# One VectorE operation per item of the side queue, and constants moved by 64 bytes: a transformer block on one core

## The chip, the cores and the metric

The kernel runs on one core of one Trainium2 chip. The time is the device time of one execution in microseconds (us). The kernel before took 1429.42 us, the median of 3 runs (1429.18 to 1429.70).

## The reference

One pre-norm transformer block in fp32 over 2048 tokens of width 512: attention with 32 query heads of width 16 that share one key and one value head, then a GEGLU feed-forward of width 1792.

```python
h  = x + A(layernorm(x))    # S = 2048, D = 512
h2 = h + B(layernorm(h))    # F = 1792
# A: q = x@wq (32 heads of 16), k = x@wk, v = x@wv (one head),
#    softmax(q k^T / 4) v, then @ wo
# B: (gelu(x @ w_gate) * (x @ w_up)) @ w_down
```

## The kernel before, in words

**Products.** Dense products and scores run in fp32r, each factor split into a high part and a rest, with three products (high x high, high x rest, rest x high) summed in PSUM. For the scores the three parts lie on top of one another in 50 rows (`kaug` holds the keys, `qg` the queries, with two more rows for a bound on the score), so one matmul does all.

**Attention.** The tokens are four blocks `b` of 512 queries, each with 8 groups `g` of 4 heads and 16 key chunks `kc` of 128: 512 units, each two scores (`u` = 0, 1). `scores` (line 345) issues two matmuls for one `u`, on rows 0 to 49 and 64 to 113, which run side by side (L352), and ScalarE takes the exponential into `p` (L356). `weigh` (line 358) multiplies `p` by the values `v_sb`, four heads in four column groups (L360; the profile counts each matmul twice). After 16 chunks `evacuate` copies the sum out (`oT`, L373) and it is turned around through DRAM and divided (L389, L398 to L409).

**Dense work of the block before, woven in.** From the middle of the second block on, the loop at lines 1069 to 1093 walks 47 lists of three cycles (`CYCLES`, line 45), 141 cycles in all. In a cycle the letter s issues a score, d one step of dense work, and v (or the count at the cycle's start) products with `v_sb`. Where too little dense work is ready, the cycle is idle: it takes its `plain` letters, without d, and `before(idle)` empties the side list.

`queue_products` lists the dense products of a block: `project` (with `wo`, tiles pp), then for each of 14 chunks `f` of 128 columns `up` for gate and up (pg, pu), with `down` (pd) of chunks 0 to 3 and 4 to 7 woven in two chunks after the last of them, and the rest at the block's end. `rows(a)` (line 732) runs the list twice: `rows(0)` on partitions 0 to 63 of both factors, `rows(1)` on 64 to 127, six steps later (`LAG`). The matmuls of the two streams run side by side. A product is 12 steps (fewer for some `down`), L751. Each takes a PSUM bank from `spare`, which holds three. At its last step `done` evacuates it on VectorE: L621 copies the first half out of PSUM, L625 adds the second, L681 adds to `h` for `down`, L574 and L577 for `project`.

**The side queue.** Other VectorE work of the dense part stands in the list `later`. `side(n)` (line 540) takes up to `n` items off its front and issues them. It is called with 2 after each `done` (line 758) and once a cycle in `before` (line 1059). Its items for one `f`: `cube` (L612, L613), a marker that lets ScalarE take the tanh (L637) at the next cycle's start, `weigh_up` (L643, L644), `part` (L125, L126, which make `gh` and `gl`). `norm` and its `scale` stand in the same list. `need(b, f)` issues from the list until `f` is done, where a `down` would read it too early. The order of VectorE and SyncE instructions is that in which the program issues them (`manual_schedule`).

**The tail.** The last block's dense part (`last_dense`, line 797) runs after the attention, on all 128 rows (L781, L836), with no side queue. Its first two `w2` tiles, for chunks 0 to 3, lie in buffers of `p` (line 506), the others in the dense pool (line 508).

**Where tiles lie in SBUF.** A pool's tiles lie one after another in the order of their allocation, each partition's row rounded up to 32 bytes. The pool `const` starts at byte 16512 of a partition: `ident` (512 bytes), `power` (8), `kaug`, `v_sb`, `wo_hi`, `wo_lo`, `q2` (20), `flag` (4), `b1`, `b2`. It ends at 43904, where the pools `early` (first half) and later `dense` begin. The pool of the attention (`p`, `qg`, `oc`, `o_hi`, `o_lo`) lies at the other end, from 153568 on.

Of the kernel before, what the change touches and what calls it, by code (L numbers as in the profile page):

```python
# [9 lines left out]
F32 = mybir.dt.float32  # L10
F32R = mybir.dt.float32r
BF16 = mybir.dt.bfloat16
I32 = mybir.dt.int32
AF = mybir.ActivationFunctionType
ALU = mybir.AluOpType
# [4 lines left out]
P = 128  # L20
# [37 lines left out]
def kernel(  # L58
# [12 lines left out]
    nc = tc.nc  # L71
# [3 lines left out]
    DH = wk.shape[1]  # L75
    H = wq.shape[1] // DH
    F = w_gate.shape[1]
    T = 512
    NT = S // P
    NB = S // T  # L80
# [18 lines left out]
    const = ctx.enter_context(tc.tile_pool(name="const", bufs=1))  # L99
# [5 lines left out]
    nc.vector.memset(power[:, 0:1], -0.5)  # L105
    nc.vector.memset(power[:, 1:2], 0.5)

    kaug = const.tile([P, S], F32R, name="kaug")
    v_sb = const.tile([P, KC, 2 * DH], F32, name="v_sb")
    wo_hi = const.tile([P, DC, D], F32R, name="wo_hi")  # L110
    wo_lo = const.tile([P, DC, D], F32R, name="wo_lo")
    q2 = const.tile([H, NB + 1], F32, name="q2")


    q_d = dram.tile([H, KR, S], F32R, name="q_d")
    acc_d = dram.tile([P, 4, T], F32, name="acc_d")
# [4 lines left out]
    def split(eng_hi, hi, lo, src, eng_lo=None):  # L121
        if eng_hi is nc.scalar:
            nc.scalar.activation(hi, src, AF.Copy)
        else:
            eng_hi.tensor_copy(hi, src)  # L125
        (eng_lo or nc.vector).tensor_tensor(lo, src, hi.bitcast(F32), op=ALU.subtract)  # L126
# [21 lines left out]
    def attend(first):  # L148
        with ExitStack() as outer:
            with tc.manual_schedule(  # L150
                engines={mybir.EngineType.PE, mybir.EngineType.Pool, mybir.EngineType.Activation}
            ):
                run(outer, first)


    def run(outer, first):
# [24 lines left out]
        eb = None  # L181
        if first:
            eb = early.enter_context(tc.tile_pool(name="early", bufs=1))

            xT = {
                b: [eb.tile([P, DC, T], F32R, name=f"xT_{w}_{b}") for w in ("hi", "lo")]
                for b in range(1, NB)
            }
            wq_hi = eb.tile([P, DC, D], F32R, name="wq_hi")
            wq_lo = eb.tile([P, DC, D], F32R, name="wq_lo")  # L190
            sel = eb.tile([P, DC, H], BF16, name="sel")
            k2m = eb.tile([H, 1], F32, name="k2m")


        def project_q(b, cs, eng, col):
# [126 lines left out]
        if first:  # L322
            set_banks("ps_pro")
            width = 8
            order = tc.manual_schedule(engines={mybir.EngineType.DVE})
            with order:
                qg_first = prologue(
                    psum1, xT, wq_hi, wq_lo, sel, k2m, q_first, q_rest, advance,
                    first_q, first_bound, eb
                )  # L330
        sb = outer.enter_context(tc.tile_pool(name="attn", bufs=1, side="right"))
# [163 lines left out]
        def load_w1(i):  # L495
            b, m = divmod(i, 2 * FC)
            if b == NB:
                return
            f, k = divmod(m, 2)
            w = db.tile([P, 2, DC, P], F32R, tag="w1", bufs=3, name=f"w1_{b}_{f}_{k}")  # L500
            nc.sync.dma_start(w.bitcast(F32), w1_d[f, k].bitcast(F32))
            w1s[b, f, k] = w
# [19 lines left out]
        scaled_at, halves, gs, gated = {}, {}, {}, set()  # L522
        tanhs, later = [], []
# [21 lines left out]
        def product_terms(parts):  # L545
            return [
                (l, r, f)
                for f, (lh, ll), (rh, rl) in parts
                for l, r in ((lh, rh), (lh, rl), (ll, rh))
            ]  # L550
# [49 lines left out]
        def up(b, f, k):  # L600
            def terms():
                w = w1s.pop((b, f, k))
                hi, lo = xTs[b]
                return product_terms([
                    (None, (w[:, 0, c, :], w[:, 1, c, :]), (hi[:, c, :], lo[:, c, :]))
                    for c in range(DC)
                ])

            def cube():
                g, a = halves[b, f, 0], db.tile([P, T], F32, tag="ga", bufs=2, name=f"ga_{b}_{f}")  # L610
                halves[b, f, 2] = a
                nc.vector.tensor_tensor(a, g, g, op=ALU.mult)  # L612
                nc.vector.scalar_tensor_tensor(  # L613
                    a, a, 1.0 / GELU_A, g, op0=ALU.add, op1=ALU.mult
                )

            def done(a, bank):
                tag = "gu"[k]
                if a == 0:
                    half = db.tile([P, T], F32, tag=tag, bufs=2, name=f"{tag}_{b}_{f}")  # L620
                    nc.vector.tensor_copy(half, bank)  # L621
                    halves[b, f, k] = half
                else:
                    half = halves[b, f, k]
                    nc.vector.tensor_tensor(half, half, bank, op=ALU.add)  # L625
                    load_w1(b * 2 * FC + 2 * f + k + 3)
                    if k == 0:
                        later.append(cube)
                    else:
                        later.append(lambda: tanhs.append((b, f)))  # L630

            ready = (lambda: turned.get(b, 0) == TB) if f == 0 and k == 0 else None
            return f"p{'gu'[k]}_{b}_{f}", 3 * DC, terms, done, ready

        def bend(b, f):
# [3 lines left out]
        def gate(b, f):  # L639
            g, u, a = (halves.pop((b, f, k)) for k in range(3))  # L640

            def weigh_up():
                nc.vector.scalar_tensor_tensor(a, a, 1.0, g, op0=ALU.add, op1=ALU.mult)  # L643
                nc.vector.tensor_tensor(a, a, u, op=ALU.mult)  # L644

            def part():
                key = b, f // 2
                if key not in gs:
                    gs[key] = [
                        db.tile([P, 2, T], F32R, tag=tag, bufs=3, name=f"{tag}_{b}_{f // 2}")  # L650
                        for tag in ("gh", "gl")
                    ]
                gh, gl = gs[key]
                split(nc.vector, gh[:, f % 2, :], gl[:, f % 2, :], a)
                gated.add((b, f))

            return [weigh_up, part]

        def need(b, f):
            while (b, f) not in gated:  # L660
                if later:
                    side(1)
                else:
                    key = tanhs.pop(0)
                    bend(*key)
                    later.extend(gate(*key))
# [402 lines left out]
        for i in range(-((lead - end) // 16)):  # L1069
            if first and i in BOUND_LISTS:  # L1070
                bound_flag(BOUND_LISTS.index(i))
            for count, woven, plain in CYCLES:
                idle = available() < woven.count("d")
                if idle:
                    while available():
                        step()
                    if at == len(queue) or queue[at][0].startswith("pg"):
                        catch_up()
                bent = before(idle)
                if not idle:  # L1080
                    finish(count)
                for key in bent:
                    later.extend(gate(*key))
                for move in plain if idle else woven:
                    if move == "d":
                        step()
                    elif move == "v":
                        finish(1)
                        clock += 4
                    elif n < end:  # L1090
                        score(n)
                        n += 1
                        clock += 1
# [24 lines left out]
    def prologue(psum1, xT, wq_hi, wq_lo, sel, k2m, q_first, q_rest, advance, first_q, first_bound, eb):  # L1118
        with ExitStack() as pro:
            sb = pro.enter_context(tc.tile_pool(name="pro", bufs=1))  # L1120
            xT[0] = [sb.tile([P, DC, T], F32R, name=f"xT_{w}_0") for w in ("hi", "lo")]

            warm = sb.tile([P, 1], F32, name="warm")
            nc.scalar.activation(warm, power[:, 1:2], AF.Copy)

            wkv = sb.tile([P, DC, 2 * DH], F32, name="wkv")
# [196 lines left out]
            b = NB - 1  # L1323
# [18 lines left out]
                advance(q_rest, 3 * DC * (DC - FIRST_Q) - 21)  # L1342
            return qg

    flag = const.tile([1, 1], I32, name="flag")
    b1 = const.tile([1, 1], F32, name="b1")
    b2 = const.tile([1, H], F32, name="b2")
    b_d = dram.tile([1, H], F32, name="b_d")
# [83 lines left out]
```

## Time and profile before

| What | Value |
|---|---|
| median of 3 runs | 1429.42 us |
| the profiled execution's own time | 1433.01 us |
| its span, first to last instruction | 1430.9 us |
| granted TensorE clock, mean | 0.997 |
| VectorE instructions, busy | 1043, 639.4 us |
| POOL busy | 219.4 us |

The profile is of one execution. Its page has the busy time of each engine (PE is TensorE's matmuls, PEld its weight loads, DVE VectorE, ACT ScalarE, POOL GpSimd), the chain of work that ended last, and the costliest groups of instructions: line, engine, operation, `out<-in` by the tiles' names, the count, busy time and mean length, then the idle time just before them and what ended it. Matmuls are pipelined and their ends are modelled, so a busy PE may still lose time; it is seen in the distance from one start to the next. The trace answers further questions: who waited for whom, the instructions in order of time, the chain in order of time, and the groups of a stretch.

### The profile page before, as it was taken

How to read it: one execution, taken by the hardware profiler on the slowest of the kernel's cores; microseconds unless marked ns; L12 is line 12 of the kernel's file. 1: busy time of each engine (PE TensorE's matmuls, PEld its weight loads, DVE VectorE, ACT ScalarE, POOL GpSimd, SP SyncE). 2: the span in 40 equal slices, each digit the busy share in tenths (PEclk: the TensorE clock that was granted, in tenths of full speed). 3: DMA queues.
4: the chain of work that ended last, by engine and by line, in shares of the span. 5: the costliest groups of instructions: out<-in, count | busy, mean ns of one | idle time of the engine just before them, and what ended most of it. 6: DMA issues, size and time to landing. Idle time of an engine off the chain costs nothing.

```text
span 1430.9 us, 25109 instructions
## 1 busy us (share of the span) xinstructions
PE 1396.5 (98%) x10384; PEld 752.4 (53%) x10384; DVE 639.4 (45%) x1043; ACT 1031.6 (72%) x1147; POOL 219.4 (15%) x305
## 2 busy tenths in 40 slices
PE   6999999999999999999999999999999999999998
PEld 5433333335455555545555555545555555556876
DVE  7413131224364444455364444545354453436665
ACT  7699999997877777877777777777777777752000
POOL 5587767710000000000000000000000000001000
PEclk9999999999999999999999999999999999999999
DMA  4467667634222332312422333311332333244352
GB/s 157 140 204 237 222 216 222 226 103 177 71 90 89 111 116 101 108 64 63 168 82 78 131 101 107 108 49 42 147 101 86 115 112 104 89 148 175 126 185 76
DMA packets 66930, 180.57 MB, mean 126 GB/s; under 512 B 9436, under 2 KB 9436, under 8 KB 66776
## 3 DMA queue, kind: packets, MB, share of 16 engines
q1 hardware_dynamic: 56976, 144.79, 30.4%
q0 software_dynamic: 9760, 34.08, 7.1%
q8 instruction: 84, 1.38, 0.4%
q14 instruction: 38, 0.31, 0.1%
q10 hardware_dynamic: 72, 0.00, 0.0%
HBM read 131.13 MB, written 47.71 MB: 125 GB/s over the span
## 4 chain that ended last, share of the span: by engine, by line
PE 89%; DVE 4%; ACT 3%; DMA 1%; issue 1%; SPq 0%; ACTq 0%; DVEq 0%
PE acc L360 31%; PE s L352 19%; PE pg L751 8%; PE pd L751 8%; PE pu L751 7%; PE pq L205 4%; ACT p L356 3%; PE pd L781 3%; PE pp L751 2%; PE pu L781 2%; PE pg L781 2%; DMA w<-w_d 1%; PE pk L1219 1%; PE pd_rest L793 1%; DVE ga L644 0%
## 5 line engine op out<-in xcount | busy, mean ns | idle before, releaser
L356 ACT ACTIVATE p<-s 128x1024 f32<-128x1024 f32 x1024 | 960.8, 1039 | 241.2 <-PE s L352 240.9
L360 PE MATMUL acc<-p,v_sb 128*32 128x512 f32 x4096 | 492.6, 601 | 0.0
L352 PE MATMUL s<-qg,kaug 50*128 50x512 f32 x1984 | 389.8, 427 | 4.1 <-ACT p L356 3.6
L352 PEld LDWEIGHTS s<-qg,kaug 50*128 50x128 f32 x1984 | 171.6, 184 | 286.8 <-issue 133.0
L360 PEld LDWEIGHTS acc<-p,v_sb 128*32 128x32 f32 x4096 | 110.1, 109 | 231.7 <-issue 217.3
L751 PE MATMUL pg<-x2h,w 64*128 64x512 f32 x672 | 177.1, 394 | 4.2 <-DVE g L625 3.1
L751 PE MATMUL pu<-x2h,w 64*128 64x512 f32 x672 | 175.6, 393 | 0.0
L135 POOL TENSOR_SCALAR rstd<-mv 128x1 f32<-128x1 f32 x16 | 3.5, 220 | 977.9 <-DVE mv L133 977.8
L751 PE MATMUL pd<-w,gh 64*128 64x512 f32 x624 | 124.1, 392 | 1.4 <-DVE h L681 1.4
L681 DVE TENSOR_TENSOR h<-h,pd 128x512 f32<-128x512 f32 x80 | 54.4, 686 | 149.4 <-PE pd L751 149.4
L751 PEld LDWEIGHTS pg<-x2h,w 64*128 64x128 f32 x672 | 95.8, 185 | 20.3 <-DVE g L625 6.5
L751 PEld LDWEIGHTS pu<-x2h,w 64*128 64x128 f32 x672 | 94.7, 185 | 11.4
L751 PE MATMUL pg<-x2l,w 64*128 64x512 f32 x336 | 100.3, 391 | 0.0
L751 PE MATMUL pu<-x2l,w 64*128 64x512 f32 x336 | 99.2, 391 | 0.0
L751 PEld LDWEIGHTS pd<-w,gh 64*128 64x128 f32 x624 | 68.4, 185 | 13.1 <-DVE h L681 2.7
L890 ACT ACTIVATE ga<-ga 128x512 f32<-128x512 f32 x14 | 8.8, 632 | 92.0 <-DVE ga L887 92.0
L389 DVE RECIPROCAL oc<-oc 128x128 f32<-128x128 f32 x64 | 56.6, 922 | 34.2 <-DMA oc<-acc_d 33.8
L751 PE MATMUL pd<-w,gl 64*128 64x512 f32 x312 | 71.8, 391 | 0.0
L625 DVE TENSOR_TENSOR g<-g,pg 128x512 f32<-128x512 f32 x42 | 28.7, 684 | 91.0 <-PE pg L751 91.0
L625 DVE TENSOR_TENSOR u<-u,pu 128x512 f32<-128x512 f32 x42 | 28.9, 687 | 78.7 <-PE pu L751 78.5
L621 DVE COPY g<-pg 128x512 f32<-128x512 f32 x42 | 29.0, 691 | 74.7 <-PE pg L751 74.7
L125 DVE CAST qh<-pq 128x512 fp32r<-128x512 f32 x11 | 7.6, 689 | 114.4 <-PE pq L205 114.4
(242 smaller groups left out, 1477.7 us busy)
## 6 DMA issues: line engine op xcount, KB each, us to landing
w<-w_d SPq DMA_DIRECT2D x112, 512.0 KB
w<-w_d SPq DMA_DIRECT2D x28, 1024.0 KB
qg<-q_d SPq DMA_DIRECT2D x62, 200.0 KB
q_d<-qh SPq DMA_DIRECT2D x32, 256.0 KB
acc_d<-oT SPq DMA_DIRECT2D x32, 256.0 KB
oc<-acc_d SPq DMA_DIRECT2D x128, 64.0 KB
w_d<-w_0b POOLq DMA_DIRECT2D x14, 512.0 KB, 3.8
w_d<-w_1b POOLq DMA_DIRECT2D x14, 512.0 KB, 5.6
```

The lines of the kernel that those rows point to most:

```text
L205: nc.tensor.matmul(pq, wt[:, d, c * P : (c + 1) * P], xt[:, d, :], start=(n == 0), stop=(n == 3 * DC - 1),)
L352: nc.tensor.matmul(s[:, a, :], kaug[rows, kc * P : (kc + 1) * P], qg[rows, u, :], start=True, stop=True,)
L356: nc.scalar.activation(p[:, 2 * u : 2 * u + 2, :], s, AF.Exp, scale=SCALE)
L360: nc.tensor.matmul(acc[32 * j : 32 * j + 32, :], v_sb[:, kc, :], p[:, j, :], start=(kc == 0), stop=(kc == KC - 1), skip_group_check=True,)
L389: nc.vector.reciprocal(oc[:, 1, sl], oc[:, 1, sl])
L621: nc.vector.tensor_copy(half, bank)
L625: nc.vector.tensor_tensor(half, half, bank, op=ALU.add)
L681: nc.vector.tensor_tensor(hs[b, t], hs[b, t], bank, op=ALU.add)
L751: nc.tensor.matmul(bank, lhsT[r], rhs[r], start=(k == 0), stop=(k == n - 1), skip_group_check=True,)
L781: nc.tensor.matmul(bank, lhsT, rhs, start=(i == 0), stop=(i == len(ts) - 1))
L793: nc.tensor.matmul(bank, lhsT, rhs, start=(i == 0), stop=(i == len(ts) - 1))
L1219: nc.tensor.matmul(pks[b], wt[:, c, :], xt[:, c, :], start=(c == 0 and n == 0), stop=(c == DC - 1 and n == 2),)
```

## The change

Two things are changed.

First, the side queue. `cube` becomes two items, `square` (the old L612) and `cube` (L613); `weigh_up` becomes `bring` (L643) and `weigh_up` (L644); `part` becomes `high` (L125) and `low` (L126). Each item is one VectorE operation. `side` still takes two items a call.

Second, the order and width of small tiles. `q2` and `flag` are allocated ahead of `kaug`; `k2m` and `warm` are made 64 bytes wider in the pool, with only their first column used, and `warm` is allocated ahead of `xT[0]`. No instruction is added or removed.

```diff
+    q2 = const.tile([H, NB + 1], F32, name="q2")
+    flag = const.tile([1, 1], I32, name="flag")
     kaug = const.tile([P, S], F32R, name="kaug")
     v_sb = const.tile([P, KC, 2 * DH], F32, name="v_sb")
     wo_hi = const.tile([P, DC, D], F32R, name="wo_hi")
     wo_lo = const.tile([P, DC, D], F32R, name="wo_lo")
-    q2 = const.tile([H, NB + 1], F32, name="q2")
...
-            k2m = eb.tile([H, 1], F32, name="k2m")
+            k2m = eb.tile([H, T // 32 + 1], F32, name="k2m")[:, :1]
...
-            def cube():
+            def square():
                 g, a = halves[b, f, 0], db.tile([P, T], F32, tag="ga", bufs=2, name=f"ga_{b}_{f}")
                 halves[b, f, 2] = a
                 nc.vector.tensor_tensor(a, g, g, op=ALU.mult)
+
+            def cube():
+                g, a = halves[b, f, 0], halves[b, f, 2]
                 nc.vector.scalar_tensor_tensor(
                     a, a, 1.0 / GELU_A, g, op0=ALU.add, op1=ALU.mult
                 )
...
-                        later.append(cube)
+                        later.extend((square, cube))
...
+            def bring():
+                nc.vector.scalar_tensor_tensor(a, a, 1.0, g, op0=ALU.add, op1=ALU.mult)
+
             def weigh_up():
-                nc.vector.scalar_tensor_tensor(a, a, 1.0, g, op0=ALU.add, op1=ALU.mult)
                 nc.vector.tensor_tensor(a, a, u, op=ALU.mult)
 
-            def part():
+            def high():
...
-                gh, gl = gs[key]
-                split(nc.vector, gh[:, f % 2, :], gl[:, f % 2, :], a)
+                nc.vector.tensor_copy(gs[key][0][:, f % 2, :], a)
+
+            def low():
+                gh, gl = gs[b, f // 2]
+                nc.vector.tensor_tensor(
+                    gl[:, f % 2, :], a, gh[:, f % 2, :].bitcast(F32), op=ALU.subtract
+                )
                 gated.add((b, f))
 
-            return [weigh_up, part]
+            return [bring, weigh_up, high, low]
...
+            warm = sb.tile([P, DH], F32, name="warm")[:, :1]
             xT[0] = [sb.tile([P, DC, T], F32R, name=f"xT_{w}_0") for w in ("hi", "lo")]
-            warm = sb.tile([P, 1], F32, name="warm")
...
-    flag = const.tile([1, 1], I32, name="flag")
```

## The prediction, made before the changed kernel was timed

> **What bounds the kernel now.** I read the page first: the head, the row of TensorE, and the shares of the chain that ended last.
>
> ```profile
> span 1430.9 us, 25109 instructions
> PE 1396.5 (98%) x10384; PEld 752.4 (53%) x10384; DVE 639.4 (45%) x1043; ACT 1031.6 (72%) x1147; POOL 219.4 (15%) x305
> PE 89%; DVE 4%; ACT 3%; DMA 1%; issue 1%; SPq 0%; ACTq 0%; DVEq 0%
> L356 ACT ACTIVATE p<-s 128x1024 f32<-128x1024 f32 x1024 | 960.8, 1039 | 241.2 <-PE s L352 240.9
> ```
>
> TensorE is busy 98% of the span and is 89% of the chain. ScalarE, the next busiest, spends 240.9 us waiting for TensorE's scores. VectorE has 55% of the span free. So only what delays TensorE counts, and a VectorE edit is worth what TensorE waits for VectorE. The waits of PE over the stretch in which attention and dense products are woven (300 to 1275 us) give that; columns are total us, times, longest.
>
> ```profile
> PE s L352 <- ACT p L356: 3.6, 10, 0.7
> PE pg L751 <- DVE g L625: 3.1, 8, 0.4
> PE pd L751 <- DVE h L681: 1.4, 3, 0.6
> PE pg L751 <- DVE u L621: 1.2, 2, 0.6
> ```
>
> There are thirteen waits for VectorE, eight of one kind. All are waits for a PSUM bank: three banks (`spare`) serve two streams of products, and a product's first matmul needs the bank that the last evacuation but one gave back. No row has a product waiting for `gh` or `gl`, so gated values are never late.
>
> The rows show idle time against modelled matmul ends; what a wait costs is read from the starts. This is the timeline of PE around one of the eight, then that of DVE before it (start, length, idle in brackets).
>
> ```profile
> 709.33 0.40 PE L352 MATMUL s<-qg,kaug 50*128 50x512 f32 x2
> 709.56 0.40 PE L751 MATMUL pu<-x2l,w 64*128 64x512 f32 x2
> 709.79 0.40 PE L751 MATMUL pu<-x2h,w 64*128 64x512 f32 x2
> 710.57 0.50 PE L751 MATMUL pg<-x2h,w 64*128 64x512 f32 x1 [0.37 <-DVE g L625]
> 710.57 0.50 PE L751 MATMUL pu<-x2h,w 64*128 64x512 f32 x1
> 710.91 0.40 PE L352 MATMUL s<-qg,kaug 50*128 50x512 f32 x2
> ```
>
> ```profile
> 706.71 0.69 DVE L621 COPY g<-pg 128x512 f32<-128x512 f32 x1 [0.17 <-PE pg L751]
> 707.32 0.68 DVE L643 SCALAR_TENSOR_TENSOR ga<-ga,g 128x512 f32<-128x512 f32 x1
> 708.04 0.69 DVE L644 TENSOR_TENSOR ga<-ga,u 128x512 f32<-128x512 f32 x1
> 708.76 0.43 DVE L125 CAST gh<-ga 128x512 fp32r<-128x512 f32 x1
> 709.22 0.69 DVE L126 TENSOR_TENSOR gl<-ga,gh 128x512 fp32r<-128x512 f32 x1
> 709.83 0.68 DVE L625 TENSOR_TENSOR g<-g,pg 128x512 f32<-128x512 f32 x1
> 710.55 0.69 DVE L612 TENSOR_TENSOR ga<-g 128x512 f32<-128x512 f32 x1
> ```
>
> TensorE starts a slot every 0.23 us (709.33, 709.56, 709.79). The next starts 0.78 us on, so 0.55 us are lost, and the one after it 0.34 us on, 0.11 us more: 0.65 us a wait, 5.2 us for eight. The cause stands in the second fence. The evacuation at 706.71 was followed by `side(2)`, and its two items were `weigh_up` (L643, L644) and `part` (L125, L126): four operations, 707.32 to 709.83. The evacuation of `g` (L625) stood behind them with no idle time before it, and its bank came late.
>
> **The side queue, step by step.** No operation is added or removed; the same seven an `f` keep their order among themselves and are dealt out two a call instead of up to four. In the case above the call after the copy at 706.71 now emits L643 and L644 only. L625 then starts where L125 did, at 708.76, 1.07 us earlier. The slot that lost 0.55 us lost it to L625's late end, so it is free 0.5 us before TensorE needs it: **the wait goes whole**, 0.65 us. Next in the queue come L125 and L126 (1.1 us), then the evacuation of `u`, then L612 and L613: a call puts two operations (1.4 us) ahead of the next evacuation, where it put up to four (here 2.5 us).
>
> The two waits for `u` are the same with reciprocals between. DVE, then PE, at the first:
>
> ```profile
> 723.03 0.69 DVE L625 TENSOR_TENSOR g<-g,pg 128x512 f32<-128x512 f32 x1 [2.93 <-PE pg L751]
> 723.64 0.68 DVE L643 SCALAR_TENSOR_TENSOR ga<-ga,g 128x512 f32<-128x512 f32 x1
> 724.36 0.69 DVE L644 TENSOR_TENSOR ga<-ga,u 128x512 f32<-128x512 f32 x1
> 725.08 0.43 DVE L125 CAST gh<-ga 128x512 fp32r<-128x512 f32 x1
> 725.54 0.69 DVE L126 TENSOR_TENSOR gl<-ga,gh 128x512 fp32r<-128x512 f32 x1
> 726.15 1.76 DVE L389 RECIPROCAL oc<-oc 128x128 f32<-128x128 f32 x2
> 727.83 0.63 DVE L612 TENSOR_TENSOR ga<-g 128x512 f32<-128x512 f32 x1
> 728.49 0.69 DVE L613 SCALAR_TENSOR_TENSOR ga<-ga,g 128x512 f32<-128x512 f32 x1
> 729.10 0.68 DVE L621 COPY u<-pu 128x512 f32<-128x512 f32 x1
> ```
>
> ```profile
> 728.63 0.63 PE L751 MATMUL pg<-x2h,w 64*128 64x512 f32 x2
> 729.84 0.50 PE L751 MATMUL pg<-x2h,w 64*128 64x512 f32 x1 [0.58 <-DVE u L621]
> 730.18 0.62 PE L751 MATMUL pg<-x2l,w 64*128 64x512 f32 x2
> ```
>
> The last slot before is at 728.63 + 0.23 = 728.86; 0.98 us to the next and 0.34 to the one after lose 0.75 + 0.11 = 0.86 us. Now L612 and L613 come out one call later, behind the copy of `u`, which moves up by their 1.3 us. I count 0.65 us saved and leave 0.2 for what now follows the copy: 1.3 us for two. The three waits of `pd` for `h` (L681) come from products of six terms whose evacuations follow each other with no item between: unchanged.
>
> Sum: 5.2 + 1.3 = **6.5 us**; the ends are 0 (the waits only move) and 6.9 (all ten go).
>
> What could come late instead: an item is now up to one call further back, so the tanh and `gl` come later by a few microseconds. `gl` of an `f` is first read two `f` later, 48 slots of 0.23 us or more, over 11 us; at a block's end, where less work lies between, a cycle without dense work empties the list (`side(100)`). ScalarE's 240.9 us of waiting cover the tanh. Without that cover a late `gl` would stop TensorE by about what one call holds, 1.4 us, once a block: 4 us. DMAs: none is issued by an item; `load_w1` stays in `done`.
>
> **The layout.** Each tile takes its row's bytes rounded up to 32. `q2` and `flag` (32 bytes each) now lie ahead of `kaug`, so `kaug`, `v_sb`, `wo_hi` and `wo_lo` move up by 64 bytes; the same 64 are gone behind them, so the dense pool (`x2h`, `w`, `gh`, `gl`) and the attention pool (`qg`, `p`, `o_hi`) **don't move**. Row starts modulo 256: `kaug` and `wo` go from 160 to 224, which is where `qg`, `p` and `o_hi` lie; the dense pool stays at 128. `v_sb`'s chunks of 128 bytes alternate 160 and 32, now 224 and 96. In the prologue `xT[0]` goes from 0 to 128, like `wq_hi`, and `qg_first` follows `kaug`.
>
> The trace has one clean trial of such a match: in the last block the first two `w2` tiles sit in `p` buffers (224) and the others in the dense pool (128), with `gh` at 128. The chain shows the two runs of 48 matmuls, and PE's groups of each window its means (first pair of rows the mismatched, second the matched).
>
> ```profile
> 1335.26 11.21 PE pd L781 x48
> 1368.27 10.88 PE pd L781 x48
> ```
>
> ```profile
> L781 PE MATMUL pd<-w,gh 128*128 128x512 f32 x32 | 10.0, 394 | 0.0
> L781 PE MATMUL pd<-w,gl 128*128 128x512 f32 x16 | 6.4, 399 | 0.0
> L781 PE MATMUL pd<-w,gh 128*128 128x512 f32 x32 | 9.9, 389 | 0.0
> L781 PE MATMUL pd<-w,gl 128*128 128x512 f32 x16 | 6.2, 389 | 0.0
> ```
>
> The mismatch costs (11.21 - 10.88)/48 = **6.9 ns a matmul**. In the woven part, where two row groups run side by side, the mismatched `pp` and the matched `pd` take the same; these rows, and those of S and PV, are the page's groups.
>
> ```profile
> L751 PE MATMUL pp<-wo_hi,o_hi 64*128 64x512 f32 x96 | 21.7, 392 | 0.0
> L751 PE MATMUL pd<-w,gh 64*128 64x512 f32 x624 | 124.1, 392 | 1.4 <-DVE h L681 1.4
> L836 PE MATMUL pp<-wo_hi,o_lo 128*128 128x512 f32 x16 | 6.3, 395 | 0.0
> L352 PE MATMUL s<-qg,kaug 50*128 50x512 f32 x1984 | 389.8, 427 | 4.1 <-ACT p L356 3.6
> L360 PE MATMUL acc<-p,v_sb 128*32 128x512 f32 x4096 | 492.6, 601 | 0.0
> ```
>
> Certain gainers are the 48 alone-running `pp` of the tail (395 against 389): 0.3 us. S following S, one a cycle in 141 cycles, could gain up to 141 x 6.9 ns = 1.0 us; I take half, because the paired `pp` shows nothing. S beside dense products stays mismatched (224 against 128). The prologue's products wait for other engines. I take **0.8 us**. The ends: all 1024 slots of S (pairs of the 2048) gain or lose 6.9 ns, 7.1 us either way; for the PV quads (1024) see the last rival.
>
> [...]
>
> **Sum.** The profiled execution took 1433.01 us, 2.1 outside its 1430.9 of span. 1433.01 - 6.5 - 0.8 = 1425.7. The median of the runs is 3.59 us lower, 1429.42, and the waits recur with the program's order, so I take the same 7.3 us off it: **1422.1 us**.
>
> **Rivals.**
> - The layout does nothing (paired `pp` 392 like `pd` 392; against it 11.21 and 10.88): 1429.42 - 6.5 = 1422.9.
> - The layout does all it might for S, 7.1 us in place of 0.8: 1415.8. Against it: S stays mismatched with the dense products around it.
> - The waits move: a late `gl` once a block (4 us), or the ten waits return at other banks. For it: the list holds more items at a time. Against it: VectorE has idled 2.9 us shortly before the burst (723.03). 1429.42 - 6.5 + 4 = 1426.9, with the layout at 0; whole, 1429.4.
> - Slower: the 64 bytes turn against S and PV. Place: the weight loads of `kaug` and `v_sb` beside 1024 S slots and 1024 PV quads. Price: the tail's 6.9 ns on each of the 2048, 14.1 us: 1429.42 - 6.5 + 14.1 = 1437.0. It passes the time before from 6.5/2048 = 3.2 ns on, and by 0.2% from 4.6 ns. For it: PV's remainders 224 and 96 are tried nowhere in this trace. Against: in the one clean trial the match is the faster.
>
> **How the numbers follow.** Chances: forecast 0.46; layout nothing 0.25; layout large 0.07; waits move 0.12; the slower rival 0.10. The range leaves out the last and most of the large layout: 1417.5 to 1429.0. A measurement of this kernel can tell about 0.2% from no change, 2.9 us. Below 1426.6: the first three and a little of the fourth, 0.80; within 0.2%: the rest of the fourth, 0.10; slower 0.10.
>
> **What would show it.** Right: the eight waits of `pg` for `g` L625 and the two for `u` L621 are gone from PE's waits while the three for `h` stay; on DVE L643 and L644 no longer run straight into L125 and L126 ahead of L625; the tail's `pp` falls from 395 towards 389 and its first 48 `pd` keep 11.21. Wrong: new waits of `pd` for `gl` or of ScalarE's tanh; or the gain is there and PV or S starts further apart than before. The forecast fails if banks are late for another reason than the burst, or if S's spacing changes in the woven part, either way.

## The result, and the profile after

The changed kernel takes **1423.57 us** (median of 7 runs, 1421.93 to 1425.77) against 1429.58 us for the kernel before (7 runs): a ratio of 0.9957, 95% interval 0.9946 to 0.9968, which is 4.6 to 7.7 us faster. The forecast was 1422.1 us in a range of 1417.5 to 1429.0.

The profiled execution took 1423.57 us, the median itself. Its page, the rows that answer to those of before:

```profile
span 1421.5 us, 25079 instructions
PE 1392.2 (98%) x10384; PEld 752.6 (53%) x10384; DVE 635.9 (45%) x1043; ACT 1030.0 (72%) x1147; POOL 217.0 (15%) x305
PE 93%; ACT 2%; DVE 2%; DMA 1%; issue 1%; POOL 0%; SPq 0%; DVEq 0%; ACTq 0%; POOLq 0%
L356 ACT ACTIVATE p<-s 128x1024 f32<-128x1024 f32 x1024 | 959.5, 1040 | 233.8 <-PE s L352 233.5
```

The engines' counts are as before (the 30 instructions fewer in the head are VectorE's semaphore instructions, 230 for 260), and TensorE is still the bound; VectorE's share of the chain falls from 4% to 2%. PE's waits from 290 to 1275 us (total us, times, longest):

```profile
PE s L352 <- ACT p L356: 3.5, 10, 0.6
PE pd L761 <- DVE h L691: 1.4, 3, 0.5
PE pxt L587 <- issue: 0.3, 1, 0.3
```

The eight waits of `pg` for `g` and the two for `u` are gone, and no new row has come: the kernel before has the row of `pxt` too, 0.2 us. (The change moves line numbers: L751 is now L761, L625 is L628, L643 and L644 are L646 and L649, L125 and L126 of the gate are L658 and L662.) VectorE's timeline at the place that the prediction showed, then PE's:

```profile
706.13 0.69 DVE L624 COPY g<-pg 128x512 f32<-128x512 f32 x1 [0.17 <-PE pg L761]
706.74 0.68 DVE L646 SCALAR_TENSOR_TENSOR ga<-ga,g 128x512 f32<-128x512 f32 x1
707.46 0.69 DVE L649 TENSOR_TENSOR ga<-ga,u 128x512 f32<-128x512 f32 x1
708.07 0.68 DVE L628 TENSOR_TENSOR g<-g,pg 128x512 f32<-128x512 f32 x1
708.67 0.42 DVE L658 CAST gh<-ga 128x512 fp32r<-128x512 f32 x1
709.12 0.69 DVE L662 TENSOR_TENSOR gl<-ga,gh 128x512 fp32r<-128x512 f32 x1
709.73 0.69 DVE L624 COPY u<-pu 128x512 f32<-128x512 f32 x1
```

```profile
708.97 0.40 PE L761 MATMUL pu<-x2l,w 64*128 64x512 f32 x2
709.21 0.40 PE L761 MATMUL pu<-x2h,w 64*128 64x512 f32 x2
709.44 0.40 PE L761 MATMUL pg<-x2h,w 64*128 64x512 f32 x1
709.44 0.40 PE L761 MATMUL pu<-x2h,w 64*128 64x512 f32 x1
709.67 0.40 PE L352 MATMUL s<-qg,kaug 50*128 50x512 f32 x2
```

L628 now starts 1.94 us after the copy of `g`, where it stood 3.12 us behind it (706.71 to 709.83). TensorE keeps its 0.23 us a slot: 708.97, 709.21, 709.44, 709.67. At the first wait for `u` its copy now comes ahead of L612 and L613 (L616 in this kernel), as forecast:

```profile
725.81 0.69 DVE L662 TENSOR_TENSOR gl<-ga,gh 128x512 fp32r<-128x512 f32 x1
726.42 0.68 DVE L624 COPY u<-pu 128x512 f32<-128x512 f32 x1
727.02 0.68 DVE L612 TENSOR_TENSOR ga<-g 128x512 f32<-128x512 f32 x1
```

**Where the time went, by stretch.** Both kernels issue the same 2048 score matmuls in the same order, so their starts in the trace are milestones. The last row is from the last score to the span's end.

| Stretch (score matmuls, from 0) | before, us | after, us | difference |
|---|---|---|---|
| 0 to 128 | 65.36 | 66.85 | +1.49 |
| 128 to 512 | 185.96 | 186.03 | +0.07 |
| 512 to 640 | 76.50 | 74.98 | -1.52 |
| 640 to 2047 (all ten waits) | 893.99 | 885.26 | -8.73 |
| after the last score | 156.50 | 156.04 | -0.46 |

The two profiles differ by 9.4 us of span, the medians by 6.0. The first and the third row are not the change's: they are single stretches of 3.41 us at a granted clock of 0.50 (clock windows from here on; the last section shows them), and executions of one kernel differ in the clock (mean of an execution 0.996 to 0.999 in 29 runs of the kernel before). The last row holds one too, in the changed kernel alone (granted clock 0.83 from 1279 to 1289 us), so its -0.46 us says little. The profiled execution of before (1433.01 us) lies 3.43 us above its median, that of the changed kernel on its median; this is the difference between 9.4 and 6.0.

### The profile page after: what moved, and what is told of

It is laid out like the page before. It is cut to its first block, busy times and chain, and to the rows that moved or that the text cites. A ratio compares the mean times of both kernels' runs of the same rounds, so it can differ in the third digit from the quotient of the medians.

```text
span 1421.5 us, 25079 instructions
## 1 busy us (share of the span) xinstructions
PE 1392.2 (98%) x10384; PEld 752.6 (53%) x10384; DVE 635.9 (45%) x1043; ACT 1030.0 (72%) x1147; POOL 217.0 (15%) x305
## 4 chain that ended last, share of the span: by engine, by line
PE 93%; ACT 2%; DVE 2%; DMA 1%; issue 1%; POOL 0%; SPq 0%; DVEq 0%; ACTq 0%; POOLq 0%
PE acc L360 32%; PE s L352 20%; PE pg L761 8%; PE pu L761 8%; PE pd L761 8%; PE pq L205 3%; PE pd L791 3%; PE pp L761 3%; PE pu L791 2%; PE pg L791 2%; ACT p L356 2%; PE pd_rest L803 1%; PE pxt L587 0%; DMA w<-w_d 0%; PE pk L1229 0%
## 5 line engine op out<-in xcount | busy, mean ns | idle before, releaser
L761 PE MATMUL pg<-x2h,w 64*128 64x512 f32 x672 | 173.9, 392 | 0.0
L761 PE MATMUL pu<-x2h,w 64*128 64x512 f32 x672 | 172.5, 391 | 0.0
L761 PE MATMUL pd<-w,gh 64*128 64x512 f32 x624 | 123.9, 392 | 1.4 <-DVE h L691 1.4
L761 PEld LDWEIGHTS pg<-x2h,w 64*128 64x128 f32 x672 | 94.3, 185 | 11.5
L761 PEld LDWEIGHTS pu<-x2h,w 64*128 64x128 f32 x672 | 94.2, 185 | 11.5
L761 PE MATMUL pg<-x2l,w 64*128 64x512 f32 x336 | 99.2, 391 | 0.0
L761 PE MATMUL pu<-x2l,w 64*128 64x512 f32 x336 | 98.8, 391 | 0.0
L761 PEld LDWEIGHTS pd<-w,gh 64*128 64x128 f32 x624 | 68.3, 185 | 13.3 <-DVE h L691 2.7
L761 PE MATMUL pd<-w,gl 64*128 64x512 f32 x312 | 71.7, 391 | 0.0
L628 DVE TENSOR_TENSOR g<-g,pg 128x512 f32<-128x512 f32 x42 | 28.8, 685 | 90.5 <-PE pg L761 90.5
L628 DVE TENSOR_TENSOR u<-u,pu 128x512 f32<-128x512 f32 x42 | 28.8, 686 | 68.0 <-PE pu L761 68.0
L125 DVE CAST qh<-pq 128x512 fp32r<-128x512 f32 x11 | 7.6, 690 | 113.3 <-PE pq L205 113.3
```

The costliest lines, as they stand in the source:

```text
L761: nc.tensor.matmul(bank, lhsT[r], rhs[r], start=(k == 0), stop=(k == n - 1), skip_group_check=True,)
```

## The experiments

Each kernel was timed against the kernel before on the same chip, in five rounds. The stretch from score matmul 640 to 2047, in which all ten waits lie, is given beside the ratio, since it is free of the clock windows (granted clock 1.00 from 340 us to the last score, before and after). Line numbers differ by one or a few between kernels.

**The side queue alone** (`q2`, `flag`, `k2m`, `warm` as before the change):

```diff
-    q2 = const.tile([H, NB + 1], F32, name="q2")
-    flag = const.tile([1, 1], I32, name="flag")
     kaug = const.tile([P, S], F32R, name="kaug")
...
+    q2 = const.tile([H, NB + 1], F32, name="q2")
...
-            k2m = eb.tile([H, T // 32 + 1], F32, name="k2m")[:, :1]
+            k2m = eb.tile([H, 1], F32, name="k2m")
...
-            warm = sb.tile([P, DH], F32, name="warm")[:, :1]
+            warm = sb.tile([P, 1], F32, name="warm")
...
+    flag = const.tile([1, 1], I32, name="flag")
```

> The side queue alone, tiles where they were before. Theory (the burst of four operations behind an evacuation made all ten bank waits, and they are all of the gain): 6.0 to 6.5 us faster than before, ratio about 0.9956; the eight waits of pg for g and the two for u are gone from PE's waits, the three of pd for h stay (1.4 us). Rival (the moved tiles bring part of the gain): ratio 0.997 to 0.999. Rival (the waits only move): ratio 0.999 to 1.000 and ten waits elsewhere.

Measured: 1423.32 us against 1429.61, ratio 0.9948, interval 0.9933 to 0.9962; the stretch 886.51 us. PE's waits:

```profile
PE s L351 <- ACT p L355: 3.7, 11, 0.7
PE pd L760 <- DVE h L690: 1.4, 3, 0.5
```

All of the gain that the runs can tell, and both rivals out: the ten waits are gone with the tiles where they were. At just these ten places the scores come earlier than in the kernel before, and that makes up the 7.5 us of the stretch. The changed kernel's stretch is 1.25 us shorter still; this gathers evenly, with no wait behind it, and the next experiment has the same layout with a longer stretch than before, so it stays open.

**The layout alone** (`q2`, `flag`, `k2m` and `warm` as in the changed kernel, the side queue as before):

> The moved tiles alone, the side queue as before. Theory: ratio 0.9990 to 1.0005 (0 to 1 us faster), the ten bank waits stand as before (4.3 us idle in PE's waits). Rival (layout large): ratio 0.995. Rival (the move turns against S and PV): ratio 1.002 or more, with PV's or S's starts further apart than 429 and 232 ns.

Measured: 1429.38 us, ratio 0.9993, interval 0.9984 to 1.0001; the stretch 894.50 us (893.99 before). PE's waits for VectorE:

```profile
PE pg L752 <- DVE g L626: 3.1, 8, 0.4
PE pd L752 <- DVE h L682: 1.4, 3, 0.5
PE pg L752 <- DVE u L622: 1.2, 2, 0.6
```

The layout is no difference that the runs can tell. The large layout and the slower rival are both out.

**Only the constants** (`q2` and `flag` ahead of `kaug`; nothing else):

> Only q2 and flag ahead of the keys (kaug, v_sb, wo up by 64 bytes), nothing in the prologue's pools moved. Theory: ratio 0.999 to 1.000; in the tail the pp matmuls fall from 395 to 389 ns (0.3 us), S and PV unchanged in the woven part. Rival (the 1.5 us that the changed kernel lost between its first and its 128th score come from kaug and v_sb): ratio 1.000 to 1.001 and the 1.5 us show here.

Measured: 1428.85 us, ratio 0.9991, interval 0.9980 to 1.0002. The stretch is 894.28 us, and the first 128 scores take 65.33 us (65.36 before). The groups of the tail's `pp`:

```profile
L837 PE MATMUL pp<-wo_hi,o_lo 128*128 128x512 f32 x16 | 6.3, 392 | 0.0
L837 PE MATMUL pp<-wo_lo,o_hi 128*128 128x512 f32 x16 | 6.2, 391 | 0.0
```

They fall from 395 to 391.5 ns, 3 to 4 ns and not the 6 that were forecast.

**Only `k2m` and `warm`** (`k2m` takes 64 bytes more of its pool; `warm` takes 64 in place of 32, so 32 more, and stands ahead of `xT[0]`):

> Only k2m and warm widened (tiles of the first pools moved), constants in place. Theory: ratio 0.9995 to 1.0005, since the first part waits on loads, VectorE and ScalarE. Rival (the 1.5 us that the changed kernel lost between its first and its 128th score come from the tiles of the first pools): ratio 1.001, and the 1.5 us show here and not with the constants alone.

Measured: 1430.68 us, ratio 1.0006, interval 0.9996 to 1.0016. The first 128 scores take 66.83 us here, as in the changed kernel, which looked like the rival; but the kernel with the layout alone moves the same tiles and takes 65.28. The last section shows that it is a clock window.

**The bursts back, with fine items.** The changed kernel with four items a call:

```diff
-                        side(2)
+                        side(4)
...
-            side(100 if idle else 2)
+            side(100 if idle else 4)
```

> The changed kernel, but the list gives out four items a call in place of two: one operation an item still, and the bursts of four are back. Theory (the burst is the cause, not the form of the items): all ten bank waits are back and the gain is gone, ratio 0.999 to 1.0005. Rival (the finer items let other work in between at other places): ratio stays near 0.996.

Measured: 1428.06 us against 1429.51, ratio 0.9988, interval 0.9980 to 0.9997; the stretch 893.23 us. PE's waits for VectorE:

```profile
PE pg L761 <- DVE g L628: 3.2, 8, 0.4
PE pd L761 <- DVE h L691: 1.4, 3, 0.6
PE pg L761 <- DVE u L624: 1.2, 2, 0.6
```

All ten waits are back with one operation an item: it is how much a call issues, not the form of the items. The stretch is 8.0 us longer than the changed kernel's 885.26 on the same layout. The ratio lies just below the range expected: the median is 1.5 us below that of before, the stretch 0.8 us. What makes this is open.

**Only the gate's items split** (tiles as before, two items a call, `cube` whole):

```diff
-                        later.extend((square, cube))
+                        later.append(lambda: (square(), cube()))
```

> Tiles as before; only the gate's two items are split into four (bring, weigh_up, high, low), square and cube stay one item. Theory: this holds all of the gain, since the eight waits for g stand behind weigh_up and part, and the two for u are met by the same split (the cube comes a call later): ratio 0.995 to 0.996. Rival (the two waits for u hang on the cube): they stay, 1.7 us less gain, ratio 0.9965.

Measured: 1422.51 us, ratio 0.9950, interval 0.9937 to 0.9963; the stretch 886.27 us; the ten waits gone. This holds all of the gain.

**Only `cube` split** (tiles as before, two items a call):

```diff
-            return [bring, weigh_up, high, low]
+            return [lambda: (bring(), weigh_up()), lambda: (high(), low())]
```

> Tiles as before; only cube is split into square and cube, the gate's items stay as before. Theory: nothing, the ten waits stay: ratio 0.9995 to 1.0005. Rival (the two waits for u hang on the cube): these two go, ratio 0.9988.

Measured: 1430.96 us, ratio 1.0005, interval 0.9997 to 1.0014; the stretch 893.98 us; the ten waits stay. Nothing, so the two waits for `u` hang on the gate's items too.

**Three items a call**, on the side queue alone:

```diff
-                        side(2)
+                        side(3)
...
-            side(100 if idle else 2)
+            side(100 if idle else 3)
```

> Tiles as before, one operation an item, three items a call. Behind the copy of g now stand bring, weigh_up and high, 0.46 us more than with two a call; the prediction said that the bank then had 0.5 us to spare. Behind the add of g come three, the two reciprocals, and three more before the copy of u: the same six as in the kernel before. Theory (what counts is the time of the operations between an evacuation and the one before it): the eight waits for g stay away, or keep under 0.1 us each, and the two for u are back, 1.05 us each: 5 us faster than before, ratio 0.9965. Rival (bursts over two operations do it all): all ten back, ratio 1.000.

Measured: 1424.30 us against 1430.07, ratio 0.9960, interval 0.9946 to 0.9974; the stretch 888.61 us, 2.10 more than with two a call. PE's waits for VectorE, and VectorE at the first wait for `u`:

```profile
PE pd L760 <- DVE h L690: 1.4, 3, 0.5
PE pg L760 <- DVE u L623: 0.9, 2, 0.5
```

```profile
719.51 0.69 DVE L627 TENSOR_TENSOR g<-g,pg 128x512 f32<-128x512 f32 x1 [2.93 <-PE pg L760]
720.11 0.69 DVE L645 SCALAR_TENSOR_TENSOR ga<-ga,g 128x512 f32<-128x512 f32 x1
720.83 0.69 DVE L648 TENSOR_TENSOR ga<-ga,u 128x512 f32<-128x512 f32 x1
721.56 0.43 DVE L657 CAST gh<-ga 128x512 fp32r<-128x512 f32 x1
721.90 1.76 DVE L388 RECIPROCAL oc<-oc 128x128 f32<-128x128 f32 x2
723.58 0.63 DVE L661 TENSOR_TENSOR gl<-ga,gh 128x512 fp32r<-128x512 f32 x1
724.12 0.68 DVE L611 TENSOR_TENSOR ga<-g 128x512 f32<-128x512 f32 x1
724.83 0.69 DVE L615 SCALAR_TENSOR_TENSOR ga<-ga,g 128x512 f32<-128x512 f32 x1
725.44 0.68 DVE L623 COPY u<-pu 128x512 f32<-128x512 f32 x1
```

Just the two waits for `u` are back, 1.05 us each, and the eight for `g` stay away. The copy of `u` stands behind the same eight operations (six of the list, two reciprocals) as in the kernel before; behind the copy of `g` stand three. So it is not the number of items a call that decides: with the same three a call, the eight stay away and the two come back. What counts is the time ahead of an evacuation against the time until its bank is wanted, as the theory had it.

**A mismatch put in.** The changed kernel with 160 unused bytes in the dense pool, between `x2l` and the rest:

```diff
+            if b == 0:
+                db.tile([P, 40], F32, tag="gap", bufs=1, name="gap")
```

> The changed kernel with an unused tile of 160 bytes between x2l and the rest of the dense pool: x2 stays at 128 modulo 256, the weights w go to 32, so that gate and up products are mismatched as the first 48 pd of the tail were. If a mismatch costs 6.9 ns a matmul only where products run alone: the tail's 336 gate and up matmuls take 2.3 us more (234 in place of 227 ns each), the woven ones the same; 2.3 us slower than the changed kernel, ratio to before 0.997. If it costs everywhere: 1008 woven slots more, 9.3 us slower than the changed kernel, ratio 1.002. [...]

Measured: 1423.47 us against 1429.51, ratio 0.9954, interval 0.9940 to 0.9968. The chain in the tail, and the groups of the woven products from 340 to 1260 us:

```profile
1337.88 2.80 PE pg L793 x12
1340.68 2.80 PE pu L793 x12
```

```profile
L763 PE MATMUL pg<-x2h,w 64*128 64x512 f32 x672 | 174.3, 392 | 0.0
L763 PE MATMUL pu<-x2h,w 64*128 64x512 f32 x672 | 173.3, 392 | 0.0
```

In the tail a gate or up product of 12 takes 2.80 us, against 2.72 in the changed kernel: (2.80 - 2.72)/12 = 6.7 ns a matmul, 2.2 us over 28 products, the price of the natural trial once more. In the woven part the means are 392 as in the changed kernel (392 and 391), and the stretch is 885.91 us against 885.26: 0.65 us more over 1008 slots, where 6.9 ns each would make 7.0, and no more than the stretches of kernels without the ten waits differ by (885.26 to 886.51). The tail's 2.2 us do not show in the median, whose runs spread over 3.4 us; by the ratio alone, 0.9954 beside the changed kernel's 0.9957, the addresses would do nothing. From the last score to the end the profile has 157.17 us, against 154.56 to 156.50 in the eleven others.

**All matched.** The changed kernel with 96 unused bytes ahead of the dense pool, and `k2m` and `warm` wider to suit, so that `kaug`, `v_sb`, `wo`, `qg`, `p` and every dense tile start at 224 modulo 256:

```diff
-            k2m = eb.tile([H, T // 32 + 1], F32, name="k2m")[:, :1]
+            k2m = eb.tile([H, T // 8], F32, name="k2m")[:, :1]
...
-            warm = sb.tile([P, DH], F32, name="warm")[:, :1]
+            warm = sb.tile([P, DH + 24], F32, name="warm")[:, :1]
...
+    const.tile([P, 24], F32, name="pad")
```

> The changed kernel with 96 bytes of padding before the dense pool (and k2m and warm widened to suit), so that constants, attention tiles and dense tiles all start at 224 modulo 256, S and dense products with each other too. Theory (in the woven part addresses are worth nothing, alone 6.9 ns a matmul): the tail's first 48 pd take 10.88 us in place of 11.21, the woven part is within 1 us of the changed kernel: ratio 0.995 to 0.996. Rival (S beside dense products pays for its mismatch): some 880 slots beside each other gain 2 to 7 ns, 2 to 6 us faster than the changed kernel, ratio 0.992 to 0.994.

Measured: 1421.92 us against 1430.07, ratio 0.9940, interval 0.9927 to 0.9954; the stretch 885.53 us. The chain at the tail's three runs of `pd`:

```profile
1324.13 10.88 PE pd L791 x48
1356.77 10.88 PE pd L791 x48
1395.44 16.33 PE pd L791 x72
```

The first 48 take 10.88 us in place of 11.21, as forecast; the woven stretch is the changed kernel's to 0.3 us. Its ratio lies in the rival's range and not in the theory's, but the rival's 2 to 6 us would have to show in the stretch, and there they are not. It has the lowest median of all, but its interval overlaps that of the changed kernel, so it isn't shown to be faster by more than the 0.33 us of the tail.

## Why the prediction was right, point by point

- **What bounds it.** Right: TensorE, and from VectorE only its bank waits. Ten went and three stayed, as listed.
- **The eight waits for `g`.** Right in cause and size. Forecast 0.65 us each. At the eight places the lead of the side queue alone over the kernel before grows by 0.62 to 0.70 us from one score to the next, 5.3 us together. That the bank then has 0.5 us to spare held as far as tried: 0.46 us more of operations in front brought none of the eight back.
- **The two waits for `u`.** Right in cause, under-sized: this is the term that was off. Forecast 0.65 us each, measured 1.05 (2.10 us between two and three items a call). Two things were wrong in the 0.86 - 0.2. No wait was left behind the copy, so the 0.2 was not needed. And 0.2 us were missed: in the kernel before, the wait stopped one of the two streams after the other had already started, so that afterwards they ran a whole slot of 0.23 us apart. PE's timeline of before shows it after the wait, where the two matmuls of one score, else one row of 0.40 us, span 0.73 and 0.63:

```profile
729.84 0.73 PE L352 MATMUL s<-qg,kaug 50*128 50x512 f32 x2
730.18 0.62 PE L751 MATMUL pg<-x2l,w 64*128 64x512 f32 x2
730.41 0.86 PE L751 MATMUL pg<-x2h,w 64*128 64x512 f32 x4
730.88 0.63 PE L352 MATMUL s<-qg,kaug 50*128 50x512 f32 x2
```

  The 0.63 is 0.40 and one slot. With this slot the sum is 0.86 + 0.23 = 1.09 us, against the 1.05 measured.

- **The side queue's sum.** Forecast 6.5 us; by the waits 8 x 0.65 + 2 x 1.05 = 7.3; by the runs 6.3 (alone) and 7.0 (gate only); by the stretch 7.5 and 7.7. That the whole forecast of 7.3 us meets the waits' 7.3 is luck: it had 0.8 us too little for the waits and 0.8 us for a layout that isn't shown to give anything.
- **The layout.** Forecast 0.8 us, with 0 as the likeliest rival. Measured alone 0.2 us, interval -2.3 to +0.1 us: not to be told from either. What can be told is where the trial of the tail holds. Where a product runs alone, a mismatch costs 6.7 to 6.9 ns a matmul, put in (2.80 us for 12) or taken out (10.88 us for 48). In the woven part nothing was found: 392 ns with the gap and 392 without. The half of 1.0 us that I gave to the scores is therefore not supported, and of the 0.3 us for the tail's `pp` about half came, 395 to 391.5 ns, read where only the constants move, since a clock window lies over them in the changed kernel (granted clock 0.83 from 1279 to 1289 us). Its first 48 `pd` keep 11.21 us, as forecast. With `w` at 224 these take 11.21 beside `gh` at 128 and 10.88 beside `gh` at 224, so it is the two addresses together that count; why, and whether 256 is the right modulus, no run shows.
- **The rivals.** No wait moved: no row of `pd` for `gl` and none for the woven part's tanh came up in any run. No run was slower than before by more than its interval.
- **The time.** 1422.1 forecast, 1423.57 measured. The 7.3 us forecast are within the measured 4.6 to 7.7; the 1.5 us between the two are no more than one clock window (1.49 and 1.52 us in the table of stretches).

## What to carry to other kernels

When a bounding engine waits for buffers that another engine empties, look at what stands in that engine's queue between two evacuations, and weigh its time against the time until the buffer is wanted: an engine that is 45% busy can still be late by a burst. Items of unlike length hide this: here two items a call were up to four operations, and issuing two operations a call moved the late evacuations up by 1 us and more and took ten waits away. Weigh the time per call, not the items: three a call were short enough in eight places and too long in two. Where two streams share an engine side by side, a wait that hits one of them can cost more than its gap, since they go on out of step (here 1.05 us in place of 0.86).

## What the runs showed of the hardware that was not expected

The executions of one kernel differ by up to 6.5 us (the kernel before, 1427.89 to 1434.42 us in 29 runs), and a part of that comes in steps. The granted clock (PEclk, third column from the end) over the same 25 us of the profile before, of the changed kernel and of the all-matched one:

```profile
55.00:80.00 25.00, 23.41 (x144) 8.32 (x143) 5.83 (x10) 21.39 (x24) 16.14 (x21) 0.93 0.57 188
```

```profile
55.00:80.00 25.00, 23.41 (x136) 7.94 (x137) 5.84 (x10) 19.90 (x22) 15.94 (x21) 0.86 0.59 188
```

```profile
55.00:80.00 25.00, 23.42 (x154) 8.55 (x156) 5.84 (x10) 22.67 (x25) 15.79 (x21) 1.00 0.60 193
```

The clock is 0.93, 0.86 and 1.00, and the first 128 scores take 65.36, 66.85 and 63.87 us: steps of 1.5 us for 0.07 of 25 us, which is 1.75 us of clock. In the profile before the clock is 0.50 from 61.18 to 64.59 us and 1.00 on both sides. All twelve profiles stand on one of these steps: 63.9 us in three, 65.3 in seven, 66.8 in two. The same stands behind the third row of the stretches: from 300 to 340 us the profile before has 0.96 and the changed kernel 1.00, for 1.52 us. That is why the run with `k2m` and `warm` alone seemed to lose 1.5 us at the start (its clock there is 0.86 as well). It is not why the two profiles differ by more than the medians: the changed kernel's has one such window more than that of before, three against two ahead of the last 20 us (in its profile the clock is 0.50 from 60.09 to 66.90 us, two windows long, and from 1282.06 to 1285.46; in that of before from 61.18 to 64.59 and from 310.36 to 313.76). The rows from 300 to 340 us, before and after:

```profile
300.00:340.00 40.00, 38.29 (x270) 14.69 (x270) 10.18 (x17) 34.94 (x38) 1.64 (x6) 0.96 0.50 182
```

```profile
300.00:340.00 40.00, 38.29 (x286) 15.06 (x281) 10.64 (x18) 36.43 (x40) 2.01 (x6) 1.00 0.51 183
```

At a clock of 0.50 a window of 3.41 us has 1.7 us of full clock less, an estimate from these two numbers; the steps of 1.75 us and of 1.6 us (0.04 of 40) agree with it. What sets the clock to 0.50, and in which executions a window falls so, was not tried.
